# One decode layer on one core: q computed by rows, and the odd rows of w2 loaded first, three to a packet

## The chip, the cores and the metric

The kernel runs on one core of one Trainium2 chip. The metric is the device time of one execution in microseconds, the median of three runs. Engines are named as in the profile: PE (matrix products), PEld (its weight loads), DVE (vector), ACT (activation and copies), POOL, and SP, which here only issues transfers. Sixteen DMA engines of the core move the data.

## The reference

A decode step for four sequences, one token each: layer norm, attention with a cache of 4096 keys and values for 32 heads of 128, output projection and residual, then layer norm and a dense block with the activation h * tanh(softplus(h)), and a second residual.

```python
def _A_ref(x, k_cache, v_cache, wq, wo):      # x: 4 x 1 x 640, caches: 4 x 32 x 4096 x 128, bf16
    q = (x @ wq).reshape(B, Sq, H, Dh) ...
    scores = jnp.einsum("bhqd,bhkd->bhqk", q, k_cache) * (Dh ** -0.5)
    p = _softmax(scores, axis=-1)
    o = jnp.einsum("bhqk,bhkd->bhqd", p, v_cache)
    return o ... @ wo

def _B_ref(x, w1, b1, w2):                    # w1: 640 x 1728, w2: 1728 x 640
    h = jnp.einsum("bsd,df->bsf", x, w1) + b1
    sp = jnp.log1p(jnp.exp(-jnp.abs(h))) + jnp.where(h > 0, h, jnp.zeros_like(h))
    act = h * jnp.tanh(sp)
    return jnp.einsum("bsf,fd->bsd", act, w2)

h = x + _A_ref(_layernorm(x, axis=-1), A_k_cache, A_v_cache, A_wq, A_wo)
h2 = h + _B_ref(_layernorm(h, axis=-1), B_w1, B_b1, B_w2)
```

The two caches are 268 MB of the 283 MB that are read.

## The kernel before

The work is cut into 16 units (`NU`): a unit is one sequence and eight heads, 8 MB of keys and 8 MB of values. A load puts 256 cache rows of 128 numbers on each of 128 partitions, one packet of 64 KB for each partition (`load_kv`, L359). There are three slots of that size (`slot`, L302); unit u's keys lie in slot `slot_of(u)`, and keys and values of successive units take the slots in turn.

**Order.** Every instruction is added by hand to a list (`Program.add`, L41), with the names that it reads and writes; the program derives the waits from these and gives each engine its instructions in the order in which they were added. The units 1 to 15 run in loops on PE, DVE and ACT (`emit`, L196); what stands before and behind is straight code. All bulk transfers are issued by SP, in the order of the list: wq, K0, K1, V0, K2, V1, K3 and so on to V15 in two halves, then wo in two parts, w1 in three (`W1P`), then w2. A transfer into a slot waits in SP's queue until the slot's readers are done, and everything behind it on SP waits too. x and b1 are loaded by ACT.

**Start.** wq lies in slot 0 with x, the normalised rows `ln1_bf` and b1 behind it (L374 to L379). The normalised rows are turned on PE into `xT`, 128 x 5 x 4 (`turn_rows`, L481). `q_all` (L543) makes q with 160 products: for each of 32 heads and five chunks of 128 rows, wq is the stationary side (128 x 128) and `xT` moves (4 columns). ACT copies the result to `qT` (L559), 128 (index in the head) x 128 (head and sequence). For each unit, `q_broadcast` (L582) spreads eight of its columns over the partitions into a `qb`, which DVE multiplies with the keys (`times_q`, L637); PE sums the products (`sums`, L648). V0 goes to slot 0, after the readers of x, b1, `ln1` and wq (L613 to L617). Four PSUM banks, `s_bank`, hold the scores.

**End.** wo and w1 go to slot 0 after the last keys have been read, w2 to slot 1 after the products with V14 (`last_pv`). w2 has 1728 rows, thirteen blocks of 128 and 64 rows more (`C2`, `FREM`). Blocks 0 to 11 are loaded in pairs, two rows side by side in a packet of 2560 bytes, block 12 alone with 1280 bytes a packet; the parts are blocks 0 to 5, 6 to 9, 10 and 11, and 12 (`W2P`, L291). The 64 rows left go first, onto the odd partitions of a tile `w2r_sb` that POOL has cleared (L895 to L906). Their part of the activations sits with 64 rows of block 12 in a chunk that overlaps it (`f_rows`, L533); a product with `apart` (L1154) picks it out and spreads it onto the odd partitions, and ACT copies it to `act_r` (L1158).

`h1_pass` (L1051) makes the hidden layer in 5 x 14 products, a chain on DVE and ACT makes `act_t`, and `w2_products` (L1135) multiplies it with w2 in four column groups of 160: the residual first, then blocks 0 to 5, the 64 rows, and the other blocks as they land. DVE and ACT copy the four groups to `out_bf`, and SP stores it (L1175).

Of the kernel before, what the change touches and what calls it, by code (L numbers as in the profile page):

```python
# [8 lines left out]
BF16 = mybir.dt.bfloat16  # L9
ACT = mybir.ActivationFunctionType  # L10
# [224 lines left out]
def kernel(  # L235
# [13 lines left out]
    nc = tc.nc  # L249

    B, Sq, D = A_x.shape
    _, H, Sk, Dh = A_k_cache.shape
    F = B_w1.shape[1]
    N = B * Sq
    DC = D // 128
    G = 8
    PH = 128 // G
    R = Sk // PH
    NO = H // G
    NU = NO * N  # L260
# [15 lines left out]
    CT = 128 // (G * RQ)  # L276
    VQ = 2

    C2 = F // 128
    FM = C2 * 128  # L280
    FREM = F - FM
    FC = C2 + 1
    W2P = (0, 6, 10, 12, C2)
    W1P = (0, 2, 4, DC)
    OT4 = 4
    DT = D // OT4
    OVER = 128 - FREM


    pad = -int(nc.sbuf_base) % 512  # L290
# [11 lines left out]
    slot = [slots.tile([128, SLOT], BF16, name=f"slot{i}") for i in range(NS)]  # L302
    banks = [ps.tile([128, 512], FP32, name=f"bank{i}") for i in range(8)]
    s_bank, tr_bank, qq_bank, o_bank, oT_bank = banks[0:4], *banks[4:8]
    S_BANK, TR, QQ, OB, OT = [("bank", i) for i in range(4)], *[("bank", i) for i in range(4, 8)]

    def const(shape, dt, name):
        return consts.tile(shape, dt, name=name)

    ident = const([128, 128], BF16, "ident")  # L310
# [9 lines left out]
    qT = const([128, (NU + 1) * G], BF16, "qT")  # L320
# [4 lines left out]
    dq_m = const([128, Dh // J], BF16, "dq_m")  # L325
    j_f = const([128, J], FP32, "j_f")
    j_m = const([128, J], BF16, "j_m")
    xT = const([128, DC, N], BF16, "xT")
    xT_res = const([128, DC, N], FP32, "xT_res")
    qx = const([128, G, PH], BF16, "qx")  # L330
    qbs = [const([128, Dh], BF16, f"qb{i}") for i in range(NS)]
# [14 lines left out]
    P = Program(nc, tc, 1, NU - 1, NS)  # L346
# [4 lines left out]
    def cells(i, lo=0, hi=SLOT):  # L351

        return [("slot", i, p, k) for p in range(lo // PART, -(-hi // PART)) for k in range(NQ)]
# [5 lines left out]
    def load_kv(what, rows, u, i, parts=1):  # L359
        w = SLOT // parts  # L360
        for k in range(parts):
# [12 lines left out]
    first = slot[0]  # L374
    wq_sb = first[:, 0 : DC * H * Dh].rearrange("p (c n) -> p c n", c=DC)
    o0 = DC * H * Dh
    x_bf = first[0:N, o0 : o0 + D]
    ln1_bf = first[0:N, o0 + D : o0 + 2 * D]
    b1_row = first[0:1, o0 + 2 * D : o0 + 2 * D + F]  # L379
    rest0 = cells(0, o0 - o0 % PART, SLOT)  # L380

    P.add("ACT", lambda: nc.scalar.dma_start(out=x_bf, in_=x_rows[:, :]), w=["x"], sem="x")
# [3 lines left out]
        w=cells(0, 0, o0),  # L386
        sem="wq",
# [4 lines left out]
        w=["b1"],  # L392
        sem="b1",
# [9 lines left out]
            out=ident[:, :],  # L403
            in_=ident[:, :],
# [6 lines left out]
        r=["ident"],  # L411
        w=["ident"],
# [4 lines left out]
        r=["ident"],  # L417
        w=["ident_f"],
# [12 lines left out]
    def bn_stats():  # L431
        for s in range(2):
# [7 lines left out]
        r=["stats"],  # L440
        w=["mv"],
# [4 lines left out]
            out=ln_std[:, :], in_=ln_mv[:, 1:2], func=ACT.Sqrt, bias=eps_t[0:N, :], scale=1.0  # L446
        ),
        r=["mv", "eps"],
        w=["std"],
# [4 lines left out]
        r=["std"],  # L454
        w=["rstd1"],
# [4 lines left out]
            out=ln1_bf,  # L460
# [6 lines left out]
        r=["x", "mv", "rstd1"],  # L467
        w=["ln1"],
# [10 lines left out]
    tp_ps = oT_bank[:, 0 : DC * N].rearrange("p (c n) -> p c n", c=DC)  # L479

    def turn_rows(src):  # L481
# [3 lines left out]
            )  # L485
        return ins

    for src, dst, r, w in (
        (lambda c: ln1_v[:, c, :], xT, "ln1", "xT"),
        (lambda c: x_bf[:, d_rows(c)], xT_res, "x", "xT_res"),  # L490
    ):
        P.add("PE", lambda src=src: turn_rows(src), r=[r, "ident"], w=[OT])
        P.add(
            "DVE",
            lambda dst=dst: nc.vector.tensor_copy(out=dst[:, :, :], in_=tp_ps[:, :, :]),
            r=[OT],
            w=[w],
        )


    def identity_sums(dst, pattern, name, **kw):
# [15 lines left out]
        r=["own1"],  # L517
        w=["own"],
# [7 lines left out]
        r=["dq_f"],  # L526
        w=["dq_m"],
# [3 lines left out]
    )  # L531

    def f_rows(c):  # L533
        if c < C2 - C2 % 2:
            f0 = c // 2 * 256 + c % 2
            return slice(f0, f0 + 255, 2)
        f0 = c * 128 if c < C2 else F - 128
        return slice(f0, f0 + 128)


    qT_ps = qq_bank[:, 0 : N * H].rearrange("p (b h) -> p b h", b=N)

    def q_all():  # L543
        for h in range(H):
            for c in range(DC):
                ins = nc.tensor.matmul(  # L546
                    qT_ps[:, :, h],
                    lhsT=wq_sb[:, c, h * Dh : (h + 1) * Dh],
                    rhs=xT[:, c, :],
                    start=(c == 0),  # L550
                    stop=(c == DC - 1),
                )
        return ins

    P.add("PE", q_all, r=[*cells(0, 0, o0), "xT"], w=[QQ])
    P.add("DVE", lambda: nc.vector.memset(qT[:, NU * G :], 0.0), w=["qT"])
    P.add(
        "ACT",
        lambda: nc.scalar.copy(  # L559
            out=qT[:, 0 : NU * G].rearrange("p (o b g) -> p b o g", o=NO, b=N),  # L560
            in_=qT_ps[:, :, :].rearrange("p b (o g) -> p b o g", o=NO),
        ),
        r=[QQ],
        w=["qT"],
# [45 lines left out]
        )  # L610


    for x in ("x", "b1", "ln1"):  # L613
        for d in (P.writer[x], *P.readers.get(x, {}).values()):
            for cell in rest0:
                P.readers.setdefault(cell, {}).setdefault((x, d.nth), d)
# [245 lines left out]
    wo_view = A_wo.rearrange("(w p j) n -> p w j n", w=NW, j=J)  # L862
    nw2 = FC * D
    w2_sb = wend2[:, 0 : C2 * D].rearrange("p (k n) -> p k n", k=C2)
    w2r_sb = wend2[:, C2 * D : nw2]
    C2E = C2 - C2 % 2
    w2_view = B_w2[0 : C2E * 128, :].rearrange("(m p k) n -> p m (k n)", p=128, k=2)

    def load(out_ap, in_ap, i, lo, hi, name, sem=None):


        ops = {}
        for cell in cells(i, lo, hi):
            for d in P.readers.get(cell, {}).values():
                ops[d.nth] = d
        P.add(
            "SP",
            lambda: nc.sync.dma_start(out=out_ap, in_=in_ap),  # L878
            w=[name],
            sem=sem or "_".join(map(str, name)),  # L880
            after=ops.values(),
        )
# [3 lines left out]
    for k0, k1 in zip(W1P, W1P[1:]):  # L886
# [5 lines left out]
            nwo + k1 * F,  # L892
            ("w1", k0),
        )
    P.add(  # L895
        "POOL",
        lambda: nc.gpsimd.memset(w2r_sb, 0.0),
        w=["w2r"],
        after=[last_pv],
    )  # L900
    P.add(
        "SP",
        lambda: nc.sync.dma_start(out=w2r_sb[1::2, :], in_=B_w2[FM:F, :]),
        w=["w2r"],
        sem=f"slot{i2}",
    )  # L906
    for k0, k1 in zip(W2P, W2P[1:]):
        if k0 < C2E:
            assert k0 % 2 == k1 % 2 == 0
            to = wend2[:, k0 * D : k1 * D].rearrange("p (m n) -> p m n", n=2 * D)  # L910
            of = w2_view[:, k0 // 2 : k1 // 2]
        else:
            to, of = w2_sb[:, k0, :], B_w2[k0 * 128 : k1 * 128, :]
        load(to, of, i2, k0 * D, k1 * D, ("w2", k0))

    at = [nw2]
# [1 line left out]
    def scratch(n, dt=FP32):  # L918
        a = at[0]
        w = n * (2 if dt == FP32 else 1)  # L920
        w += w % 2
        at[0] = a + w
        ap = wend2[:, a : a + w]
        return ap.bitcast(FP32)[:, 0:n] if dt == FP32 else ap[:, 0:n]

    def do(eng, emit, r=(), w=()):

        return P.add(eng, emit, r=r, w=w, after=[last_pv])

    def tt(out_, a, b, op, r, w):  # L930
        do("DVE", lambda: nc.vector.tensor_tensor(out=out_, in0=a, in1=b, op=op), r, w)


    apart = scratch(128, BF16)
    do("POOL", lambda: nc.gpsimd.memset(apart, 0.0), w=["apart"])
    do(
        "POOL",
        lambda: nc.gpsimd.tensor_copy(out=apart[:, 1::2], in_=ident[:, OVER:128]),
        ["ident", "apart"],
        ["apart"],  # L940
    )


    yT = s_bank[0][:, 0 : DC * N].rearrange("p (c n) -> p c n", c=DC)
# [106 lines left out]
    def h1_pass(dc):  # L1051
        for c in range(FC):
            ins = nc.tensor.matmul(
                h1_ps[:, c, :],
                lhsT=w1_sb[:, dc, f_rows(c)],
                rhs=h2T[:, dc, :],
                start=(dc == 0 and c == 0),
                stop=(dc == DC - 1 and c == C2),
            )
        return ins  # L1060

# [72 lines left out]

    def w2_products(blocks):  # L1135
        for c in blocks:
            w2, h = (w2_sb[:, c, :], act_t[:, c, :]) if c < C2 else (w2r_sb, act_r)
            for t in range(OT4):
                ins = nc.tensor.matmul(
                    y2[32 * t : 32 * t + N, :],  # L1140
                    lhsT=h,
                    rhs=w2[:, t * DT : (t + 1) * DT],
                    start=False,
                    stop=(c == C2 - 1),
                )
        return ins

    do("PE", residual, ["hT", "ident_f"], [S_BANK[1]])

    act_r = scratch(N, BF16)  # L1150
    r_ps = oT_bank[:, 0:N]
    do(
        "PE",
        lambda: nc.tensor.matmul(r_ps, lhsT=apart, rhs=act_t[:, C2, :], start=True, stop=True),  # L1154
        ["apart", "act"],
        [OT],
    )
    do("ACT", lambda: nc.scalar.copy(out=act_r, in_=r_ps), [OT], ["act_r"])  # L1158
    for k0, k1 in zip(W2P, W2P[1:]):
        do("PE", lambda b=range(k0, k1): w2_products(b), [("w2", k0), "act"], [S_BANK[1]])  # L1160
        if k0 == 0:
            do("PE", lambda: w2_products([C2]), ["w2r", "act_r"], [S_BANK[1]])
    out_bf = scratch(D, BF16)[0:N, :]

    def gather(t, copy):
# [55 lines left out]
```

## Time and profile before

| what | value |
|---|---|
| median of 3 runs | 665.03 us (664.89 to 667.58) |
| the profiled execution's own time | 665.04 us |
| its span, first to last instruction | 663.3 us |
| granted PE clock, mean | 0.817 |
| PE busy | 381.9 us (58%) |
| DVE busy | 352.4 us (53%) |
| ACT busy | 89.2 us (13%) |
| read from memory | 283.35 MB, 427 GB/s over the span |

The span is the time between the first and the last instruction that the profiler saw; about 1.7 us of an execution lie around it. Busy times of engines are for work alone; issuing a transfer is not counted. A line such as `L639 DVE ... out<-in` is a group of instructions by source line, engine and the names of the tiles. The trace also holds a record of each DMA packet (start, duration, bytes) and the time of each semaphore increment with which an engine reports that its share of a transfer is there.

### The profile page before, as it was taken

How to read it: one execution, taken by the hardware profiler on the slowest of the kernel's cores; microseconds unless marked ns; L12 is line 12 of the kernel's file. 1: busy time of each engine (PE TensorE's matmuls, PEld its weight loads, DVE VectorE, ACT ScalarE, POOL GpSimd, SP SyncE). 2: the span in 40 equal slices, each digit the busy share in tenths (PEclk: the TensorE clock that was granted, in tenths of full speed). 3: DMA queues.
4: the chain of work that ended last, by engine and by line, in shares of the span. 5: the costliest groups of instructions: out<-in, count | busy, mean ns of one | idle time of the engine just before them, and what ended most of it. 6: DMA issues, size and time to landing. Idle time of an engine off the chain costs nothing.

```text
span 663.3 us, 6916 instructions
## 1 busy us (share of the span) xinstructions
PE 381.9 (58%) x2804; PEld 174.1 (26%) x2804; DVE 352.4 (53%) x313; ACT 89.2 (13%) x319; POOL 2.8 (0%) x14
## 2 busy tenths in 40 slices
PE   0254868375481837548183754818375481837675
PEld 0221323132230313223031322303132230313344
DVE  2075868184573818457381845738184573818502
ACT  0102020202002020200202020020202002020211
POOL 1000000000000000000000000000000000000000
PEclk9998888879695987969598796959879695987955
DMA  9999999999999999999999999999999999999997
GB/s 380 444 439 440 439 417 419 444 431 436 435 435 431 427 443 423 443 435 431 431 431 439 427 443 435 427 431 435 439 427 439 431 431 427 443 427 439 417 421 275
DMA packets 6685, 283.52 MB, mean 427 GB/s; under 512 B 713, under 2 KB 913, under 8 KB 2066
## 3 DMA queue, kind: packets, MB, share of 16 engines
q1 hardware_dynamic: 6664, 283.35, 99.1%
q8 instruction: 8, 0.13, 0.1%
q10 hardware_dynamic: 10, 0.01, 0.0%
q14 instruction: 3, 0.02, 0.0%
HBM read 283.35 MB, written 0.01 MB: 427 GB/s over the span
## 4 chain that ended last, share of the span: by engine, by line
DMA 45%; DVE 25%; PE 19%; another core or an unknown queue 6%; issue 2%; SPq 2%; ACT 1%; DVEq 0%; POOL 0%; ACTq 0%
DMA slot<-in_A_k_cache_dram 41%; DVE slot L639 21%; PE bank L651 13%; PE bank L761 5%; DMA slot<-in_B_w_dram 3%; DVE s_sb L626 3%; SPq L878 2%; ACT e L736 1%; PE bank L719 0%; DVE mx L706 0%; DVE rl L813 0%; PE bank L697 0%; DVE otn L820 0%; DVEq L228 0%
## 5 line engine op out<-in xcount | busy, mean ns | idle before, releaser
L651 PE MATMUL bank<-slot,ident 128*128 128x512 bf16 x1024 | 274.4, 423 | 242.8 <-DVE slot L639 242.8
L639 DVE TENSOR_TENSOR slot<-slot,qb 128x4096 bf16<-128x4096 bf16 x128 | 288.3, 2284 | 153.0 <-DMA slot<-in_A_k_cache_dram 148.6
L651 PEld LDWEIGHTS bank<-slot,ident 128*128 128x128 bf16 x1024 | 101.4, 107 | 401.0 <-DVE slot L639 275.2
L626 DVE TENSOR_REDUCE s_sb<-bank 128x64 f32<-128x512 f32 x64 | 44.0, 688 | 59.1 <-PE bank L651 59.1
L736 ACT ACTIVATE e<-s_sb,nb 128x256 bf16<-128x256 f32 x128 | 63.1, 495 | 45.6 <-DVE nb L728 45.6
L761 PE MATMUL bank<-slot,e 128*32 128x512 bf16 x1024 | 61.8, 395 | 4.4 <-DMA slot<-in_A_v_cache_dram 2.6
L606 ACT CAST qb<-bank 128x128 bf16<-128x128 f32 x17 | 4.5, 266 | 307.4 <-PE bank L597 307.4
L761 PEld LDWEIGHTS bank<-slot,e 128*32 128x32 bf16 x1024 | 26.3, 99 | 37.9 <-issue 9.6
L781 ACT COPY o_sb<-bank 128x512 f32<-128x512 f32 x16 | 9.4, 586 | 183.4 <-PE bank L761 183.4
L706 DVE TENSOR_REDUCE mx<-bank 1x8 f32<-1x128 f32 x16 | 4.5, 278 | 39.9 <-PE bank L697 39.9
L736 ACT ACTIVATION_READ_ACCUMULATOR e<-s_sb,nb 128x1 f32 x128 | 23.9, 187 | 0.0
L794 PE MATMUL bank<-sel,o_sb 128*128 128x8 f32 x136 | 18.5, 262 | 0.0
L794 PEld LDWEIGHTS bank<-sel,o_sb 128*128 128x128 f32 x136 | 17.4, 200 | 0.0
L813 DVE RECIPROCAL rl<-bank 128x8 f32<-128x8 f32 x17 | 3.4, 202 | 15.3 <-PE bank L794 15.3
L546 PE MATMUL bank<-xT,slot 128*128 128x4 bf16 x160 | 4.4, 168 | 10.5 <-DMA slot<-in_A_wq_dram 10.5
L719 PE MATMUL bank<-mx,nscale 1*128 1x8 f32 x32 | 6.1, 262 | 5.9 <-DVE mx L706 5.9
L580 DVE COPY b1T<-bank 128x14 f32<-128x14 f32 x1 | 0.2, 172 | 13.8 <-PE bank L570 13.8
L792 PEld LDWEIGHTS bank<-rs,ones_f 128*128 128x128 f32 x34 | 6.5, 197 | 3.8 <-ACT o_sb L781 1.6
L719 PEld LDWEIGHTS bank<-mx,nscale 1*128 1x128 f32 x32 | 4.7, 182 | 10.6 <-DVE mx L706 10.6
L546 PEld LDWEIGHTS bank<-xT,slot 128*128 128x128 bf16 x160 | 4.3, 104 | 10.5 <-DMA slot<-in_A_wq_dram 10.5
L688 DVE TENSOR_REDUCE pm<-s_sb 128x1 f32<-128x256 f32 x16 | 6.7, 420 | 0.5
L697 PE MATMUL bank<-ident_f,pm 128*1 128x128 f32 x32 | 6.1, 272 | 1.2 <-DVE pm L688 1.2
(80 smaller groups left out, 68.2 us busy)
## 6 DMA issues: line engine op xcount, KB each, us to landing
slot<-in_A_v_cache_dram SPq DMA_DIRECT2D x2, 4096.0 KB, 44.5
slot<-in_A_wq_dram SPq DMA_DIRECT2D x1, 5120.0 KB, 15.2
slot<-in_A_wo_dram SPq DMA_DIRECT2D x2, 2560.0 KB, 32.7
slot<-in_B_w_dram SPq DMA_DIRECT2D x2, 864.0 KB, 33.1
slot<-in_B_w_dram SPq DMA_DIRECT2D x1, 960.0 KB, 30.4
slot<-in_B_w_dram SPq DMA_DIRECT2D x1, 640.0 KB, 31.9
slot<-in_B_w_dram SPq DMA_DIRECT2D x1, 432.0 KB, 32.2
slot<-in_B_w_dram SPq DMA_DIRECT2D x1, 320.0 KB, 22.2
```

What stands on the lines that cost most here:

```text
L546: ins = nc.tensor.matmul(qT_ps[:, :, h], lhsT=wq_sb[:, c, h * Dh : (h + 1) * Dh], rhs=xT[:, c, :], start=(c == 0), stop=(c == DC - 1),)
L626: lambda: nc.vector.tensor_reduce(out=s_sb[:, part * RP : (part + 1) * RP], in_=s_bank[part][:, :].rearrange("p (r w) -> p r w", w=W), axi ...
L639: return nc.vector.tensor_tensor(out=kt, in0=kt, in1=qbs[u % NS][:, k * DQ : (k + 1) * DQ] .unsqueeze(1) .to_broadcast([128, RP, DQ]), op= ...
L651: ins = nc.tensor.matmul(s_bank[part][:, :].rearrange("p (r w) -> p r w", w=W), lhsT=ident[:, :], rhs=kt[:, :, d : d + W], start=(d == 0), ...
L688: lambda: nc.vector.tensor_reduce(out=pm[:, :], in_=s_sb[:, :], axis=AX.X, op=ALU.max),
L719: lambda: nc.tensor.matmul(nb_ps, lhsT=nscale[:, :], rhs=mx[:, :], start=True, stop=True),
L736: ins = nc.scalar.activation(out=e2[:, :, h, :], in_=s_sb[:, :].rearrange("p (g r) -> p g r", r=RQ), func=ACT.Exp, bias=nb[:, h : h + 1], ...
L761: ins = nc.tensor.matmul(o_bank[t : t + G * RQ, :], lhsT=e2[:, g, :, :], rhs=vt[:, g * RQ : (g + 1) * RQ, :], start=(g < CT), stop=(g >= N ...
L781: lambda: nc.scalar.copy(out=o_sb[:, :], in_=o_bank[:, :]),
L792: nc.tensor.matmul(l_ps, lhsT=ones_f[:, :], rhs=rss[u % NS][:, :], start=True, stop=True)
L794: ins = nc.tensor.matmul(o_ps, lhsT=o_sb[:, r * Dh : (r + 1) * Dh], rhs=sel[:, r, :], start=(r == 0), stop=(r == RQ - 1),)
L878: lambda: nc.sync.dma_start(out=out_ap, in_=in_ap),
```

## The change

It has two parts.

**q by rows.** `xT` gets 32 columns for each chunk, the four sequences and 28 columns of zeros, and becomes the stationary side; wq moves, 512 columns at a time. Four heads' worth of columns go to each of four groups of 32 partitions of a score bank, twice: `q_part(0)` into `s_bank[0]`, `q_part(1)` into `s_bank[1]`, 20 products each. ACT copies each bank to `q_rows`, bf16, in slot 0 behind b1. Eight more products (`q_turned`), with a selection `q_sel` cut from the identity, turn the rows into the old `qT` order. V0 waits for these reads too. That is 48 products for 160.

**w2's first rows.** w2 is split otherwise: its first 192 rows lie three to a partition on 64 partitions, loaded by eight transfers of eight packets of 3840 bytes, transfer p to the partitions p, p + 8, ... p + 56. Then come twelve blocks of 128, ten in pairs and two alone: parts of six blocks, four, one and one. The chunks of the hidden layer follow: twelve of 128 rows and three of which 64 rows are used, 15 for 14. The memset on POOL, `apart`, its product and `act_r` are gone; the 192 rows' three blocks are multiplied first, on 64 partitions.

```diff
-    C2 = F // 128
-    FM = C2 * 128
-    FREM = F - FM
-    FC = C2 + 1
-    W2P = (0, 6, 10, 12, C2)
+    C2 = F // 128 - 1
+    PR = 64
+    KR = (F - C2 * 128) // PR
+    FR = PR * KR
+    assert FR + C2 * 128 == F
+    FC = C2 + KR
+    C2E = C2 - 2
+    W2P = (0, 6, C2E, C2 - 1, C2)
...
-    xT = const([128, DC, N], BF16, "xT")
+    xT = const([128, DC, 32], BF16, "xT")
+    q_sel = const([128, CT, N], BF16, "q_sel")
...
+    q0 = -(-(o0 + 2 * D + F) // 64) * 64
+    q_rows = first[:, q0 : q0 + H * Dh // CT]
...
+    P.add("DVE", lambda: nc.vector.memset(xT[:, :, :], 0.0), w=["xT"])
+    P.add(
+        "DVE",
+        lambda: nc.vector.tensor_copy(
+            out=q_sel[:, :, :],
+            in_=ident[:, :].rearrange("p (t r) -> p t r", t=CT)[:, :, 0:N],
+        ),
...
     def f_rows(c):
-        if c < C2 - C2 % 2:
-            f0 = c // 2 * 256 + c % 2
+        if c < C2E:
+            f0 = FR + c // 2 * 256 + c % 2
             return slice(f0, f0 + 255, 2)
-        f0 = c * 128 if c < C2 else F - 128
-        return slice(f0, f0 + 128)
+        if c < C2:
+            return slice(FR + c * 128, FR + (c + 1) * 128)
+
+        return slice(c - C2, c - C2 + 127 * KR + 1, KR)
...
-    def q_all():
-        for h in range(H):
-            for c in range(DC):
+    HC = G * Dh // 512
+
+    def q_part(k):
+        for c in range(DC):
+            for t in range(CT):
+                lo = t * G * Dh + k * 512
                 ins = nc.tensor.matmul(
-                    qT_ps[:, :, h],
-                    lhsT=wq_sb[:, c, h * Dh : (h + 1) * Dh],
-                    rhs=xT[:, c, :],
+                    s_bank[k][32 * t : 32 * t + 32, :],
+                    lhsT=xT[:, c, :],
+                    rhs=wq_sb[:, c, lo : lo + 512],
                     start=(c == 0),
                     stop=(c == DC - 1),
                 )
...
+    for k in range(HC):
+        P.add("PE", lambda k=k: q_part(k), r=[*cells(0, 0, o0), "xT"], w=[S_BANK[k]])
+        P.add(
+            "ACT",
+            lambda k=k: nc.scalar.copy(
+                out=q_rows[:, k * 512 : (k + 1) * 512], in_=s_bank[k][:, :]
+            ),
...
+    def q_turned():
+        for g in range(G):
+            ins = nc.tensor.matmul(
+                qT_ps[:, g],
+                lhsT=q_rows[:, g * Dh : (g + 1) * Dh],
+                rhs=q_sel[:, :, :],
+                start=True,
+                stop=True,
+            )
...
-    for x in ("x", "b1", "ln1"):
+    for x in ("x", "b1", "ln1", *[("qrows", k) for k in range(HC)]):
...
-    P.add(
-        "POOL",
-        lambda: nc.gpsimd.memset(w2r_sb, 0.0),
-        w=["w2r"],
-        after=[last_pv],
-    )
-    P.add(
-        "SP",
-        lambda: nc.sync.dma_start(out=w2r_sb[1::2, :], in_=B_w2[FM:F, :]),
-        w=["w2r"],
-        sem=f"slot{i2}",
-    )
+
+    for p in range(8):
+        load(
+            w2r_sb[p::8, :],
+            B_w2[0:FR, :].rearrange("(p s) n -> p (s n)", s=KR)[p::8, :],
+            i2,
+            C2 * D,
+            nw2,
+            ("w2r", p),
+            f"slot{i2}",
+        )
...
-    apart = scratch(128, BF16)
...
     def w2_products(blocks):
         for c in blocks:
-            w2, h = (w2_sb[:, c, :], act_t[:, c, :]) if c < C2 else (w2r_sb, act_r)
+            if c < C2:
+                w2, h = w2_sb[:, c, :], act_t[:, c, :]
+            else:
+                w2, h = w2r_sb[:, (c - C2) * D : (c - C2 + 1) * D], act_t[0:PR, c, :]
...
     do("PE", residual, ["hT", "ident_f"], [S_BANK[1]])
-
-    act_r = scratch(N, BF16)
-    r_ps = oT_bank[:, 0:N]
     do(
         "PE",
-        lambda: nc.tensor.matmul(r_ps, lhsT=apart, rhs=act_t[:, C2, :], start=True, stop=True),
-        ["apart", "act"],
-        [OT],
-    )
-    do("ACT", lambda: nc.scalar.copy(out=act_r, in_=r_ps), [OT], ["act_r"])
+        lambda: w2_products(range(C2, FC)),
+        [*[("w2r", p) for p in range(8)], "act"],
+        [S_BANK[1]],
+    )
     for k0, k1 in zip(W2P, W2P[1:]):
         do("PE", lambda b=range(k0, k1): w2_products(b), [("w2", k0), "act"], [S_BANK[1]])
-        if k0 == 0:
-            do("PE", lambda: w2_products([C2]), ["w2r", "act_r"], [S_BANK[1]])
```

More of the change, by code (lines that the diff above doesn't have):

```diff
@@ L286 @@
     DT = D // OT4
-    OVER = 128 - FREM
     pad = -int(nc.sbuf_base) % 512
@@ L486, in turn_rows @@
         return ins
+    P.add("DVE", lambda: nc.vector.memset(xT[:, :, :], 0.0), w=["xT"])
[5 more added lines that the diff above has]
+        ),
+        r=["ident"],
+        w=["q_sel"],
+    )
     for src, dst, r, w in (
@@ L494 @@
             "DVE",
-            lambda dst=dst: nc.vector.tensor_copy(out=dst[:, :, :], in_=tp_ps[:, :, :]),
+            lambda dst=dst: nc.vector.tensor_copy(out=dst[:, :, 0:N], in_=tp_ps[:, :, :]),
             r=[OT],
@@ L533, in f_rows @@
     def f_rows(c):
-        if c < C2 - C2 % 2:
-            f0 = c // 2 * 256 + c % 2
+        if c < C2E:
+            f0 = FR + c // 2 * 256 + c % 2
             return slice(f0, f0 + 255, 2)
-        f0 = c * 128 if c < C2 else F - 128
-        return slice(f0, f0 + 128)
-    qT_ps = qq_bank[:, 0 : N * H].rearrange("p (b h) -> p b h", b=N)
-    def q_all():
-        for h in range(H):
-            for c in range(DC):
+        if c < C2:
+            return slice(FR + c * 128, FR + (c + 1) * 128)
+        return slice(c - C2, c - C2 + 127 * KR + 1, KR)
+    assert CT == NO
+    HC = G * Dh // 512
[3 more added lines that the diff above has]
+                lo = t * G * Dh + k * 512
                 ins = nc.tensor.matmul(
-                    qT_ps[:, :, h],
-                    lhsT=wq_sb[:, c, h * Dh : (h + 1) * Dh],
-                    rhs=xT[:, c, :],
+                    s_bank[k][32 * t : 32 * t + 32, :],
+                    lhsT=xT[:, c, :],
+                    rhs=wq_sb[:, c, lo : lo + 512],
                     start=(c == 0),
@@ L553, in q_all @@
         return ins
-    P.add("PE", q_all, r=[*cells(0, 0, o0), "xT"], w=[QQ])
+    for k in range(HC):
[5 more added lines that the diff above has]
+            ),
+            r=[S_BANK[k]],
+            w=[("qrows", k)],
+        )
+    qT_ps = qq_bank[:, 0 : N * H].rearrange("p (g o b) -> p g o b", g=G, o=NO)
+    def q_turned():
[7 more added lines that the diff above has]
+            )
+        return ins
+    P.add("PE", q_turned, r=[*[("qrows", k) for k in range(HC)], "q_sel"], w=[QQ])
     P.add("DVE", lambda: nc.vector.memset(qT[:, NU * G :], 0.0), w=["qT"])
@@ L559 @@
         lambda: nc.scalar.copy(
-            out=qT[:, 0 : NU * G].rearrange("p (o b g) -> p b o g", o=NO, b=N),
-            in_=qT_ps[:, :, :].rearrange("p b (o g) -> p b o g", o=NO),
+            out=qT[:, 0 : NU * G].rearrange("p (o b g) -> p o b g", o=NO, b=N),
+            in_=qT_ps[:, :, :, :].rearrange("p g o b -> p o b g"),
         ),
@@ L864 @@
     w2_sb = wend2[:, 0 : C2 * D].rearrange("p (k n) -> p k n", k=C2)
-    w2r_sb = wend2[:, C2 * D : nw2]
-    C2E = C2 - C2 % 2
-    w2_view = B_w2[0 : C2E * 128, :].rearrange("(m p k) n -> p m (k n)", p=128, k=2)
+    w2r_sb = wend2[0:PR, C2 * D : nw2]
+    w2_view = B_w2[FR : FR + C2E * 128, :].rearrange("(m p k) n -> p m (k n)", p=128, k=2)
     def load(out_ap, in_ap, i, lo, hi, name, sem=None):
@@ L894 @@
         )
-    P.add(
-        "POOL",
-        lambda: nc.gpsimd.memset(w2r_sb, 0.0),
-        w=["w2r"],
-        after=[last_pv],
-    )
-    P.add(
-        "SP",
-        lambda: nc.sync.dma_start(out=w2r_sb[1::2, :], in_=B_w2[FM:F, :]),
-        w=["w2r"],
-        sem=f"slot{i2}",
-    )
+    for p in range(8):
[7 more added lines that the diff above has]
+            f"slot{i2}",
+        )
     for k0, k1 in zip(W2P, W2P[1:]):
@@ L912 @@
         else:
-            to, of = w2_sb[:, k0, :], B_w2[k0 * 128 : k1 * 128, :]
+            to, of = w2_sb[:, k0, :], B_w2[FR + k0 * 128 : FR + k1 * 128, :]
         load(to, of, i2, k0 * D, k1 * D, ("w2", k0))
@@ L931, in tt @@
         do("DVE", lambda: nc.vector.tensor_tensor(out=out_, in0=a, in1=b, op=op), r, w)
-    apart = scratch(128, BF16)
[L935 to L940, printed above, removed]
-    )
     yT = s_bank[0][:, 0 : DC * N].rearrange("p (c n) -> p c n", c=DC)
@@ L1057, in h1_pass @@
                 start=(dc == 0 and c == 0),
-                stop=(dc == DC - 1 and c == C2),
+                stop=(dc == DC - 1 and c == FC - 1),
             )
```

## The prediction

> **What bounds the kernel now.** I read the page's slices and queue table first. The DMA row is the busy share of the 16 DMA engines in 40 slices, the last line queue SP's own share of the span.
>
> ```profile
> DMA  9999999999999999999999999999999999999997
> DMA packets 6685, 283.52 MB, mean 427 GB/s; under 512 B 713, under 2 KB 913, under 8 KB 2066
> q1 hardware_dynamic: 6664, 283.35, 99.1%
> ```
>
> The engines are full from the first slice to the last. The windows view says where that stops (us from the span's start, its length, busy time of PE, PEld, DVE, ACT, POOL, then PE clock, DMA share, GB/s):
>
> ```profile
> 36.00:626.00 590.00, 353.79 (x2216) 153.63 (x2216) 342.54 (x270) 76.28 (x285) 1.00 (x3) 0.82 1.00 433
> 657.00:658.00 1.00, 0.96 (x29) 0.87 (x29) 0.00 (x0) 0.16 (x1) 0.00 (x0) 0.50 0.85 314
> 658.00:659.00 1.00, 0.49 (x20) 0.26 (x16) 0.00 (x0) 0.00 (x0) 0.00 (x0) 0.50 0.47 170
> 659.00:660.00 1.00, 0.93 (x28) 0.27 (x16) 0.00 (x0) 0.00 (x0) 0.00 (x0) 0.50 0.03 10
> ```
>
> Share 1.00 for 590 us, then a fall over two microseconds: the 16 engines do not finish together. So the span is the time to move 283.35 MB, plus what stands before the first byte (1.5 us) and behind the last. The chain of waits, in order of time, gives that end: a w2 load, the last products, two copies (the store follows).
>
> ```profile
> 637.23 22.25 DMA slot<-in_B_w_dram
> 659.52 0.74 PE bank L1139 x9
> 660.29 0.31 DVE slot L1166
> ```
>
> The last w2 transfer's sixteen semaphore increments lie in the trace at 657.64 to 658.73 (eight) and 659.22 to 659.89 (eight). The span ends 3.4 us after the last of them (663.3 - 659.89). K and V transfers bear out the picture: from 169 to 634 us their increments repeat every 19.36 us with the same gaps between engines to about 10 ns, so no compute wait reaches the queue there, and the gaps are inherited: an engine that once served an instruction load (q8, 16 KB, eight in all) is 1.3 to 1.6 us late from then on. The chain's 25% DVE and 19% PE only say who freed a slot; another transfer was always queued behind.
>
> **Part 1, q.** The start in the timeline (start, length, then instruction and what ended the idle time before it):
>
> ```profile
> 16.00 4.43 PE L546 MATMUL bank<-xT,slot 128*128 128x4 bf16 x160 [10.45 <-DMA slot<-in_A_wq_dram]
> 20.97 0.33 SPq L365 DMA_DIRECT2D slot<-in_A_v_cache_dram  x1
> 21.44 0.27 ACT L606 CAST qb<-bank 128x128 bf16<-128x128 f32 x1 [0.38 <-PE bank L597]
> 36.03 6.70 DVE L639 TENSOR_TENSOR slot<-slot,qb 128x4096 bf16<-128x4096 bf16 x3 [14.94 <-DMA slot<-in_A_k_cache_dram]
> 630.23 3.60 PE L761 MATMUL bank<-slot,e 128*32 128x512 bf16 x32 [1.77 <-ACT e L736]
> ```
>
> Removed: 160 products, 4.43 us. Added: 40 products of 32 columns against 512. The nearest row is L761, the same shape in the same rotation over four column groups: 32 in 3.60 us after a pause, 0.1125 us each, so 40 take 4.5 us. The second of two copies of 128x512 remains behind them (L781: 0.59 us), then eight products of 128x16 (about 0.3 us; four of L967, 128x16, took 0.26), and the qT copy (0.27) that was there already. First query row ready: 21.71 + 0.1 + 0.6 + 0.3 = 22.7 us instead of 21.71. The cover is the first K load, landed at 36.0: 13 us are left. The upper bound does not break it: L651's full-width products took 0.427 us each when PE had just woken (16 in 6.1 us at 67.7), and 40 of these are 17.1 us, query row at 35.3. The lower bound is 40 at 0.056 (64 in 3.64 us at 621): 2.2 us saved. If the cover were gone, a microsecond late would still cost nothing, since V0 is the next need of the queue: SP issued it at 20.97, and K1 lands only at 54.9. V0 now also waits for the products that read the copied rows, about 21.8 us, 33 us early; behind V0 on SP stands K2, whose own wait ended at 58.45. DVE gets a memset of 128x80 and a copy of 128x16 (0.2 us each by L495's 0.18), before xT is used at 16 us. Sum of part 1: 0 to either bound.
>
> **Part 2, w2's first rows.** The tail in the timeline:
>
> ```profile
> 625.59 0.55 SPq L903 DMA_DIRECT2D slot<-in_B_w_dram  x1
> 626.18 21.97 SPq L878 DMA_DIRECT2D slot<-in_B_w_dram  x4
> 656.72 0.22 DVE L1096 SCALAR_TENSOR_TENSOR slot<-slot 128x56 bf16<-128x56 f32 x1
> 657.13 1.10 PE L1139 MATMUL bank<-slot 128*4 128x160 bf16 x28
> 658.75 1.49 PE L1139 MATMUL bank<-slot 128*4 128x160 bf16 x28 [0.51 <-DMA slot<-in_B_w_dram]
> 660.96 0.34 SPq L1175 DMA_DIRECT2D out_dram<-slot  x1
> ```
>
> Bytes stay. Packets: before 64 of 1280 B, 768 of 2560 B, 128 of 1280 B; after 64 of 3840 B, 640 of 2560 B, 256 of 1280 B. The trace's packet records give means of 55 ns (1280 B), 107 (2560), 136 (3456), 271 (6912); 3840 B by the line between the last two is 151 (estimate). Per engine, evenly spread: before 12 x 55 + 48 x 107 = 5796 ns; after 4 x 151 + 40 x 107 + 16 x 55 = 5764 ns. Nothing, then, unless the spread is uneven, and it is: x's transfer of 4 rows left four packets and five semaphore events, b1's one row one and two, the 128-row loads sixteen. So a transfer of 8 rows uses 8 engines. If all eight transfers take the same eight, these do 8 x 151 + 40 x 107 + 16 x 55 = 6368 ns plus seven more semaphore writes of 9 ns: +0.64 us; the other eight do 5160: -0.64 us.
>
> [...]
>
> What it does to the end depends on which eight. If the latest (659.89) is among them: 660.53, +0.64. If only others of the late group are: 659.50 + 0.64 = 660.14, +0.25. If they are all the early group: 658.73 + 0.64 = 659.37 against 659.89 - 0.64 = 659.25 for the others, so -0.52. In no case can PE finish before act is ready and its products done: h1 has 75 products for 70 at 30 ns (42 in 1.26 us), +0.15; act then starts PE at 657.13, the merge product L1154 (0.13 us) being gone; 60 products at 39 ns (28 in 1.10) end at 659.5 where they now end at 660.25. A gain is at most 0.8 us. I take +0.3: of the eight late engines some are likely in any half.
>
> Issues: POOL's memset, 0.63 us before L903, is gone; SP has eight issues of 0.33 to 0.55 us for one, so w2's large transfers start up to 8 x 0.55 = 4.4 us after 625.0, at 629.4 instead of 626.18. SP is held 10.37 and 9.13 us on the second and third large ones anyway, and issues the last until 648.15, 8.6 us before its first packet (656.73). The added queue entries (two per transfer on a loaded engine, 16 for 5) push that acceptance back by about 11 entries, some 3 us of drain at 271 ns: 651.2, still 5 us ahead. Behind it on SP is only the store. Cost 0; without the cover it is what exceeds 5 us.
>
> **Sum.** 663.3 + 0.0 + 0.3 = 663.6 span. The profiled execution took 665.04, 1.7 around its span, and the median of three is 665.03: 665.3.
>
> **Rivals.** *Early engines loaded:* -0.5, 664.5 (floor 664.2). For: the engine that carried b1's packet is among the early ones when its packets are followed back to back. Against: eight late engines would all have to lie in the other half. *Spread evenly after all*, so the grouping does not do what it seems: 665.0. [...] *SP held, slower than before:* if two of the eight issues were each held like the 10.37 us one, the last large transfer would be accepted at 648.2 + 20.7 = 668.9, against the 656.7 it is needed at, 12 us lost: 677. It decides from 8.6 us of hold on.
>
> **Numbers.** A difference under 0.5%, 3.3 us, cannot be told from no change here (the three runs span 2.7). Chances: late engine loaded 0.50, early ones 0.25, evenly spread 0.10, shared port 0.12, SP held 0.03. Only the last leaves the 0.5%: slower 0.04 with a little for runs like the 667.58, faster 0.01 (the floor forbids it), same 0.95. The range of 664.3 to 666.7 holds the first three cases and nearly the shared port; it leaves the SP case out.
>
> **What would show it.** After: query row at 22 to 24 us and first multiply still at 36.0; V0 issued near 22; K and V increments 19.36 us apart as before; w2's small transfers with nine semaphore events each; last increments split into a group moved by +0.64 and one by -0.64; PE still waiting for DMA in front of the last w2 block. I am wrong if the DMA share falls below 1.00 before 656, if 3840 B packets take far from 151 ns, or if the span changes by more than 2 us.

## The result, and the profile after

The changed kernel takes 667.52 us, the median of 17 runs (666.78 to 670.07); the kernel before, beside it, 665.03 (17 runs, 664.69 to 667.58). The ratio is 1.0033, 95% interval 1.0024 to 1.0043: slower by some 2.2 us, outside the prediction's range of 664.3 to 666.7. The profiled execution is one of the longer ones, 669.43 us with a span of 667.7. First the page's slices and queue table:

```profile
DMA  9999999999999999999999999999999999999996
DMA packets 6733, 283.52 MB, mean 425 GB/s; under 512 B 761, under 2 KB 1025, under 8 KB 2114
q1 hardware_dynamic: 6712, 283.35, 98.8%
```

The same bytes, and the engines as full as before. The windows view (start:end, length, busy PE, PEld, DVE, ACT, POOL, clock, DMA share, GB/s):

```profile
36.00:626.00 590.00, 349.01 (x2198) 152.24 (x2201) 341.65 (x268) 75.67 (x284) 0.00 (x0) 0.82 1.00 433
...
657.00:658.00 1.00, 0.35 (x13) 0.35 (x14) 0.00 (x0) 0.32 (x2) 0.00 (x0) 0.50 1.03 367
658.00:659.00 1.00, 1.00 (x30) 0.78 (x27) 0.44 (x2) 0.24 (x1) 0.00 (x0) 0.50 1.11 354
659.00:660.00 1.00, 0.15 (x2) 0.00 (x0) 0.89 (x3) 0.01 (x1) 0.00 (x0) 0.50 0.83 305
660.00:661.00 1.00, 0.54 (x12) 0.26 (x12) 0.28 (x2) 0.00 (x0) 0.00 (x0) 0.50 0.54 192
```

Up to 626 us nothing has moved, 433 GB/s in both kernels. The engines then empty about two microseconds later. A window around the moment when w2's first rows arrive says why; here it is for both kernels, the kernel before first:

```profile
650.00:652.00 2.00, 1.51 (x39) 1.38 (x35) 0.36 (x2) 0.00 (x0) 0.00 (x0) 0.50 1.02 405
652.00:656.00 4.00, 3.41 (x95) 3.03 (x94) 1.51 (x9) 1.89 (x4) 0.00 (x0) 0.50 1.03 395
```

```profile
650.00:652.00 2.00, 1.58 (x59) 1.59 (x60) 0.00 (x0) 0.00 (x0) 0.00 (x0) 0.50 0.99 406
652.00:656.00 4.00, 2.76 (x64) 2.54 (x62) 1.14 (x7) 0.43 (x2) 0.00 (x0) 0.50 1.06 276
```

From 652 to 656 us the engines count as busy all the time (share 1.06) and yet move 276 GB/s for 395. A busy share says that packets are open, not that bytes flow: read it beside the GB/s. The packet records show which packets were stretched (number, mean and longest ns):

```
            before                 after
1280 B      192,  55,  62          256,  59, 151
2560 B      768, 107, 281          640, 140, 260
3456 B      128, 136, 145          128, 179, 306
3840 B        -                     64, 232, 322
20480 B     256, 769, 1305         256, 768, 1305
```

The start, in the timeline of the changed kernel:

```profile
16.20 4.03 PE L565 MATMUL bank<-slot,xT 128*32 128x512 bf16 x40 [10.68 <-DMA slot<-in_A_wq_dram]
21.82 0.33 SPq L368 DMA_DIRECT2D slot<-in_A_v_cache_dram  x1
22.23 0.27 ACT L648 CAST qb<-bank 128x128 bf16<-128x128 f32 x1 [0.32 <-PE bank L639]
35.52 6.70 DVE L681 TENSOR_TENSOR slot<-slot,qb 128x4096 bf16<-128x4096 bf16 x3 [13.57 <-DMA slot<-in_A_k_cache_dram]
```

The query row is there at 22.5 us and waits 13 us for the keys. The end:

```profile
657.65 0.56 PE L1083 MATMUL bank<-slot,slot 128*128 128x4 bf16 x15 [0.79 <-DMA slot<-in_B_w_dram]
660.09 0.22 DVE L1126 SCALAR_TENSOR_TENSOR slot<-slot 128x60 bf16<-128x60 f32 x1
660.46 0.57 PE L1172 MATMUL bank<-slot 64*4 64x160 bf16 x12 [1.31 <-DVE slot L1126]
661.83 0.97 PE L1172 MATMUL bank<-slot 128*4 128x160 bf16 x24 [0.80 <-DMA slot<-in_B_w_dram]
663.48 1.16 PE L1172 MATMUL bank<-slot 128*4 128x160 bf16 x24 [0.68 <-DMA slot<-in_B_w_dram]
664.33 0.09 PEld L1172 LDWEIGHTS bank<-slot 128*4 128x4 bf16 x4 [0.34 <-DMA slot<-in_B_w_dram]
665.36 0.30 SPq L1202 DMA_DIRECT2D out_dram<-slot  x1
```

PE waits for DMA in front of the last w1 rows and of each w2 part behind the first rows, so the end is still set by the last packet. The last w2 transfer's sixteen increments lie at 659.53 to 662.68 but for one engine at 664.29, and the span ends 3.4 us later. That one engine was already 1.2 to 1.5 us behind the next in every K, V and wo transfer from 111 us on, long before w2. The other fifteen end 2.8 us after before's 659.89 (662.68); 0.4 us of that was there ahead of w2 (651.24 against 650.85 at the end of w1's first part). It is the rest that the transfers at the end have to explain.

### The profile page after: what moved, and what is told of

It is laid out like the page before. It is cut to its first block, busy times and chain, and to the rows that moved or that the text cites. A ratio compares the mean times of both kernels' runs of the same rounds, so it can differ in the third digit from the quotient of the medians.

```text
span 667.7 us, 6718 instructions
## 1 busy us (share of the span) xinstructions
PE 377.7 (57%) x2701; PEld 170.2 (25%) x2701; DVE 352.6 (53%) x315; ACT 90.3 (14%) x320; POOL 1.8 (0%) x11
## 4 chain that ended last, share of the span: by engine, by line
DMA 46%; DVE 25%; PE 19%; another core or an unknown queue 7%; issue 2%; SPq 1%; ACT 1%; DVEq 0%; ACTq 0%
DMA slot<-in_A_k_cache_dram 41%; DVE slot L681 21%; PE bank L693 13%; PE bank L803 5%; DMA slot<-in_B_w_dram 5%; DVE s_sb L668 3%; SPq L919 1%; ACT e L778 1%; PE bank L761 0%; PE bank L739 0%; DVE mx L748 0%; DVE rl L855 0%; PE bank L1172 0%; DVE otn L862 0%
## 5 line engine op out<-in xcount | busy, mean ns | idle before, releaser
L693 PE MATMUL bank<-slot,ident 128*128 128x512 bf16 x1024 | 271.2, 419 | 247.2 <-DVE slot L681 247.2
L565 PE MATMUL bank<-slot,xT 128*32 128x512 bf16 x40 | 4.0, 583 | 10.7 <-DMA slot<-in_A_wq_dram 10.7
L770 DVE TENSOR_TENSOR nb<-bank,own 128x8 f32<-128x8 f32 x16 | 2.7, 167 | 7.6 <-PE bank L761 7.6
```

The source lines that it names most:

```text
L693: ins = nc.tensor.matmul(s_bank[part][:, :].rearrange("p (r w) -> p r w", w=W), lhsT=ident[:, :], rhs=kt[:, :, d : d + W], start=(d == 0), ...
```

## The experiments

Five theories. A: two DMA engines meet where they write (the partitions decide), while w2's first rows are loaded. B: the load of eight engines is uneven, as the prediction had it. C: eight small transfers cost as such. D: the q part shifts code and instruction loads. E, added later: the rows read from memory meet, not the partitions written. Each kernel was timed beside the kernel before on the same chip, whose median lay between 664.96 and 665.28 us.

**Each part alone.** `e1_q_alone` has only the q part, `e2_w2_alone` only the w2 part:

```diff
# e1: the kernel before, with the change's q_part, q_rows, q_turned
-    P.add("PE", q_all, r=[*cells(0, 0, o0), "xT"], w=[QQ])
+    for k in range(HC):
+        P.add("PE", lambda k=k: q_part(k), r=[*cells(0, 0, o0), "xT"], w=[S_BANK[k]])
...
# e2: the changed kernel, with the old q_all
-    for k in range(HC):
-        P.add("PE", lambda k=k: q_part(k), r=[*cells(0, 0, o0), "xT"], w=[S_BANK[k]])
+    P.add("PE", q_all, r=[*cells(0, 0, o0), "xT"], w=[QQ])
```

> The kernel before with q by rows alone. Theory A (packets of two DMA engines meet on one port while w2's first rows are loaded) and theory B (the uneven load of the eight engines as such): the q part costs nothing, 664.9 to 665.2 us, ratio to before 1.000, first multiply with keys still at 35.5 to 36.0 us. Theory D (the q part shifts the code, so instruction loads fall on other DMA engines or at other times): near the changed kernel, 666.5 to 667.5.

> The changed kernel with the old q. Theories A and B: the whole loss, 666.8 to 667.5 us, the 3840-byte packets at 220 to 240 ns and the 2560-byte ones at 135 to 145 ns on the mean. Theory D: 664.9 to 665.5.

Measured: e1 664.96 us against 664.96, ratio 1.0001 (0.9990 to 1.0011); its first multiply stands at 35.56 us. e2 667.71, ratio 1.0038 (1.0025 to 1.0052), 3840-byte packets at 223 ns, 2560-byte ones at 137. D falls: the whole loss is in the w2 part.

**The same transfers to other partitions.** `e3_own_ports` keeps eight transfers of eight packets on eight engines. Only the partitions of each differ, a step of 4 for one of 8:

```diff
     for p in range(8):
+        p0 = p // 4 * 32 + p % 4
+        rows = slice(p0, p0 + 29, 4)
         load(
-            w2r_sb[p::8, :],
-            B_w2[0:FR, :].rearrange("(p s) n -> p (s n)", s=KR)[p::8, :],
+            w2r_sb[rows, :],
+            B_w2[0:FR, :].rearrange("(p s) n -> p (s n)", s=KR)[rows, :],
```

> [...] Theory A: no two engines meet, 3840-byte packets at 150 to 160 ns, 2560-byte ones at 107 to 112, time 664.4 to 665.7. Theory B or C (eight engines, or eight small transfers, whatever the partitions): packets and time as in the changed kernel, 666.8 to 667.5.

Measured: 665.25 us, ratio 1.0001 (0.9992 to 1.0011): the loss is gone. All 64 packets took 149 ns, shortest and longest alike, the 2560-byte ones 106 on the mean. Its windows in the same stretches, and the end of its chain of waits:

```profile
650.00:652.00 2.00, 1.51 (x40) 1.41 (x37) 0.36 (x2) 0.00 (x0) 0.00 (x0) 0.50 1.01 411
652.00:656.00 4.00, 3.60 (x100) 3.18 (x99) 1.40 (x8) 1.93 (x4) 0.00 (x0) 0.50 1.02 398
```

```profile
631.28 27.88 DMA slot<-in_B_w_dram
659.20 0.84 PE bank L1174 x20
660.06 0.33 PE bank L1174 x4
```

398 GB/s for 276, at about the same busy share, and the last products end 4 us ahead of the changed kernel's profiled execution (1.6 us of that is the straggler's). B and C as the main cause fall: engines, packets and transfers are as many. The 64 partitions are the same too, taken together; only which of them a transfer writes is another.

**One transfer for eight.** `e4_one_transfer` loads the 64 packets at once to partitions 0 to 63, on sixteen engines (the old load of 64 rows left sixteen increments in the kernel before):

```diff
-    for p in range(8):
+    for p in range(1):
         load(
-            w2r_sb[p::8, :],
-            B_w2[0:FR, :].rearrange("(p s) n -> p (s n)", s=KR)[p::8, :],
+            w2r_sb[:, :],
+            B_w2[0:FR, :].rearrange("(p s) n -> p (s n)", s=KR)[:, :],
```

> The changed kernel with the 64 packets of 3840 bytes in one transfer to partitions 0 to 63, so on sixteen engines, four packets each. Theory B or C: 664.9 to 665.3, packets at 151 ns. Theory A: two engines still share each port, so the 3840-byte packets stay over 200 ns, but for half as long on each engine; 665.4 to 666.6.

Measured: 666.98 us, ratio 1.0023 (1.0014 to 1.0033), 3840-byte packets at 264 ns (longest 402). That the packets stay over 200 ns is as A had it; the median lies above its range, so one transfer helped less than A allowed. An even number of packets for each engine, and one transfer, did not help on these partitions. Its window is the lowest of all:

```profile
652.00:656.00 4.00, 2.79 (x80) 2.64 (x82) 0.81 (x5) 1.75 (x3) 0.00 (x0) 0.50 1.05 225
```

**More writers on a group: a miss.** `e5_four_writers` gives each transfer eight adjacent partitions:

```diff
-            w2r_sb[p::8, :],
-            B_w2[0:FR, :].rearrange("(p s) n -> p (s n)", s=KR)[p::8, :],
+            w2r_sb[8 * p : 8 * p + 8, :],
+            B_w2[0:FR, :].rearrange("(p s) n -> p (s n)", s=KR)[8 * p : 8 * p + 8, :],
```

> [...] Theory A (engines meet on a group of partitions): four writers of w2's first rows on a group, 3840-byte packets well over the changed kernel's 232 ns, 350 to 600 ns, time 668 to 671 us. A rival by which only the number of small transfers or engines counts: 232 ns and 667 to 667.7 us as in the changed kernel.

Measured: 666.60 us, ratio 1.0021 (1.0009 to 1.0033), packets at 202 ns: less than the changed kernel, not more. The rival's 232 ns and 667 us are missed as well. The picture behind the first expectation, that the engines of one transfer write at the same moment, does not hold; the engines are 2.9 us apart when w1's last part lands (increments at 652.18 to 655.07 in this run). Of the 64 packets, 7 took 149 ns in the changed kernel, 13 in e5 and all in e3. Why e5's packets are shorter than the changed kernel's stays open; which engine writes a partition is in no trace.

**Even partitions.** `e6_even_partitions` loads all 64 packets in one transfer to the even ones of 128 partitions:

```diff
-    for p in range(8):
+    for p in range(1):
         load(
-            w2r_sb[p::8, :],
-            B_w2[0:FR, :].rearrange("(p s) n -> p (s n)", s=KR)[p::8, :],
+            wend2[0::2, C2 * D : nw2],
+            B_w2[0:FR, :].rearrange("(p s) n -> p (s n)", s=KR),
```

> The changed kernel with the 64 packets of 3840 bytes in one transfer to the 64 even partitions of all 128; the products still read partitions 0 to 63, so half of these rows of w2 are replaced by old contents and the output is not the reference's. If the engine goes with the partition, as the old load of the odd partitions suggests (1280-byte packets at 55.0 ns), the packets take 149 to 155 ns, the load is even, and the time is 664.6 to 665.1 us, at or below the run with own ports. If the engines take the 64 rows in plain order, two meet on a group as in the run with one transfer: over 200 ns, 666.3 to 667.

Measured: packets at 149 ns (longest 153), ratio 1.0004 (0.9995 to 1.0012). From 652 to 656 us the rate is 398 GB/s. So a 64-row transfer keeps the undisturbed duration when it covers all 128 partitions at a step of 2 (149 ns), and does not when it covers 64 adjacent ones (e4, 264 ns). The median, 665.74, is above what was expected; the runs spread from 664.70 to 667.12, and the profiled one, 667.12, has one engine 2.3 us behind the others at the end (661.89 against 659.60). The packets are the clearer reading here.

**Read side or write side.** `e7_src_moved` takes only the rows of e3, `e8_dst_moved` only its partitions:

```diff
# e7
-            B_w2[0:FR, :].rearrange("(p s) n -> p (s n)", s=KR)[p::8, :],
+            B_w2[0:FR, :].rearrange("(p s) n -> p (s n)", s=KR)[rows, :],
# e8
-            w2r_sb[p::8, :],
+            w2r_sb[rows, :],
```

> The changed kernel with each transfer reading the rows that the run with own ports reads, but writing partitions p, p + 8, ... as the change does; rows of w2 land on other partitions than the products expect, so the output is not the reference's. Theory A (the partitions written decide): as the changed kernel, packets 220 to 240 ns, 666.8 to 667.7 us. Theory E (the rows read from memory decide, 15360 bytes apart instead of 30720): as the run with own ports, 149 ns, 665.0 to 665.4 us.

> The other half: the changed kernel's rows read, 30720 bytes apart, written to the partitions of the run with own ports; the output is not the reference's either, for the same reason. Theory A: 149 to 155 ns, 665.0 to 665.4 us. Theory E: 220 to 240 ns, 666.8 to 667.7 us.

Measured: e7 667.37 us, ratio 1.0028 (1.0017 to 1.0039), packets at 219 ns. e8 665.20, ratio 1.0001 (0.9992 to 1.0010), all packets at 149 ns. E falls. One window of each, e7 first:

```profile
652.00:656.00 4.00, 3.04 (x75) 2.81 (x72) 1.17 (x7) 0.86 (x2) 0.00 (x0) 0.50 1.05 310
```

```profile
652.00:656.00 4.00, 3.64 (x100) 3.23 (x100) 1.35 (x8) 1.94 (x4) 0.00 (x0) 0.50 1.03 399
```

The rate follows the partitions written, whatever rows are read.

**The row that misled.** `e9_old_adjacent` is the kernel before, its one load of 64 rows put on adjacent partitions:

```diff
-        lambda: nc.sync.dma_start(out=w2r_sb[1::2, :], in_=B_w2[FM:F, :]),
+        lambda: nc.sync.dma_start(out=w2r_sb[0:64, :], in_=B_w2[FM:F, :]),
```

> The kernel before, its one load of 64 rows (1280 bytes each) put on partitions 0 to 63 instead of the 64 odd ones; the product with the activations still expects them on the odd ones, so the output is not the reference's. Theory A: the old load was free of meetings only because it covered all 128 partitions in the way of the large loads; on adjacent ones its 64 packets rise from 55 ns to 90 to 130 ns and slow the 3456- and 2560-byte packets beside them, in all some 0.3 to 0.9 us: 665.3 to 665.9 us. If small packets cannot meet, 55 ns and 665.0 us.

Measured: the 64 packets took 62.8 ns on the mean and up to 91, below the range of A; their neighbours rose more, 2560-byte packets from 107 to 115.5 and 3456-byte ones from 136 to 151. From 652 to 656 us the rate is 342 GB/s for 395:

```profile
652.00:656.00 4.00, 3.58 (x95) 3.15 (x95) 1.28 (x8) 2.00 (x4) 0.00 (x0) 0.50 1.03 342
```

The time, 666.24 us against 665.28, ratio 1.0011 (0.9999 to 1.0023), does not settle by itself. The packets do: the old load was undisturbed because of where it went; small packets are slowed too on other partitions, and their neighbours more than they.

## Why the prediction was wrong, step by step

**Where it failed.** The term of part 2 that took a 3840-byte packet for 151 ns "by the line between the last two", and every neighbour for its old duration. On the partitions of e3, e6 and e8 the size is right: 149 ns. On the partitions of the change it is 232, and the 2560-byte packets behind are 140 for 107, the 3456-byte ones 179 for 136. Spread over sixteen engines, changed kernel less e3: 1.35 us in the 2560-byte packets, 0.34 in the 3456-byte ones, 0.33 in the 3840-byte ones, 0.11 in the rest (1280 and 6912 bytes), 2.1 us in all. Against the kernel before, the packets of these sizes take 2.05 us more, and the fast end of the runs moved by 2.1 (664.69 to 666.78).

**The case that came nearest.** The chances give "shared port" 0.12. No run shows a port, there or in theory A; what the runs show in its place is that the partitions written decide (e8 149 ns, e7 219). Nor does the cost lie mainly in the loaded packets: on the mean over sixteen engines they take 0.33 us of it, and five sixths are in the packets beside them, w1's last part and w2's first. What hid it was a row of the kernel before: the 64 packets of the old odd-partition load took 55.0 ns, and that was taken as a sign that the partitions cost nothing. On partitions 0 to 63 (e9) the same packets took 62.8 ns, and their neighbours were slowed more; on the odd ones they showed nothing of the cost.

**What was right.** The bound: DMA to the last packet, 433 GB/s up to 626 us in both. Part 1 costs nothing (e1, 1.0001): 40 products in 4.03 us for an estimate of 4.5, query row at 22.5 for 22.7, V0 issued at 21.82 for 21.8, and the cover of 13 us as it stood. SP's eight issues cost 0.56 to 0.73 us each, more than the 0.33 to 0.55 assumed, and the last w2 transfer was accepted at 652.5 for 651.2; both stayed hidden, since e3 has the same issues and no loss. The eight-row transfers left nine semaphore events each. Act is ready 0.2 us later where the packets were clean (657.12 in e3 for 656.94), as the five more products of the hidden layer let expect (0.15). One reading was off without consequence: K1's last increment stands at 55.38 us, not at 54.9. And the prediction held that nothing under 0.5% could be told from no change; with 17 runs of each kernel 0.33% could.

**The uneven load.** It is there: in e3 the engines' increments lie 1.95 us apart at the end of w1 and 3.07 at the end of w2's first large part, in e6, on sixteen engines, 1.63 and 1.65 (its one late engine left out). It costs less than the +0.3 us of the forecast, or as much: the medians of e3 and e8 are 0.29 and 0.10 us above those of the kernel before beside them (665.25 and 665.20 for 664.96 and 665.10), the last increments stand at 660.02 and 659.99 against 659.89. The intervals, 0.9992 to 1.0011 and 0.9992 to 1.0010, do not separate it from nothing. Which eight engines were loaded, and whether the same ones each time, stays open.

**Left open.** The runs show that the partitions written decide, and not what lies behind them. More engines seem to be slowed than the eight with the small packets. In e2 the sixteen increments of w1's first part lie at 648.91 to 651.10 us. From there an engine without small packets needs about 5.8 us to the end of w2's first large part (an estimate from e3's means: 8 packets at 269 ns, 8 at 136, 24 at 106), and the first engine is there at 656.26. So only an engine that stood at 650.46 or later can have been undisturbed, and that is five of the sixteen, where eight carried no small packet (if the same eight carry them each time, as the spread in e3 suggests). How the slowing reaches the others is not shown. No version ran faster than the kernel before: e1 and e3 are level with it.

## What to carry to other kernels

Where DMA is the bound, look at the partitions of a small load and not at its bytes alone: with the same bytes the changed kernel took 667.52 us and e3 665.25. Try another step before giving a layout up. A full 128 partitions, every second one of them in one transfer, or eight at a step of 4 cost nothing here; 64 adjacent partitions in one transfer of 3840-byte packets, or eight at a step of 8 or side by side, took the rate from 395 GB/s to between 225 and 310 while they lasted. When a packet's duration is carried over from another load, ask whether its layout would have shown the cost at all, and price the neighbours too.

## What the runs showed of the hardware that was not expected

The busy share hides the loss: 1.06 at 276 GB/s, 1.02 at 398. The cost fell mostly on other transfers' packets, 1.8 of 2.1 us. One transfer of 64 adjacent rows, with its packets over sixteen engines, had the longest packets (264 ns) though half as many fell to each. And an engine that falls behind stays behind: in two profiled executions (669.43 us of the changed kernel, 667.12 of e6) one engine ended 1.6 and 2.3 us after the next, which is about as much as the whole change. In e6 it was 0.8 us behind up to 627 us, and 2.3 at 651, behind an instruction load of 16 KB at 634.4.
